# Block attention and a squared-ReLU MLP in one kernel: plain block products for groups 3 and 4, Strassen's scheme from group 5 on, and w_in's sums moved to VectorE

## The chip, the cores and the metric

The kernel runs on one core of one Trainium2 chip. The metric is the device time of one execution in microseconds (us), as the median of several executions. A second number is the span of one execution that was recorded by the hardware profiler; all rows of views below come from that execution.

## The reference

Two stages follow each other. Attention has 4 batches, 8 heads, 768 positions and 64 dimensions a head; a block mask lets a block of 32 queries see its neighbours, the first and last block and three sampled blocks. Its output, as 3072 rows of 512, is the input x of an MLP:

```python
h = x @ w_in                      # 3072 x 512 by 512 x 2048
r = np.maximum(h, 0.0)
g = s * (r * r) + b
return (g @ w_out).astype(np.float32)   # by 2048 x 512
```

The change concerns the MLP alone.

## The kernel before, in words

**Precision.** TensorE multiplies in a rounded format, so every operand is split into a high part (a rounded copy, made by ScalarE) and a low part (operand minus high part, made by VectorE or GpSimd), and every product is three matmuls: high by high, high by low, low by high. The weights arrive as 64-bit numbers and are decoded into the two parts by nine steps on VectorE and ScalarE (`decode_f64`, L75 to L85).

**Groups and blocks.** The 3072 rows of x make 8 groups of 384 rows, two for each batch. The hidden width 2048 makes 16 blocks f of 128. For a group g and a block f, `mlp1` (L399 to L401) makes 12 matmuls of 384 columns into a bank of PSUM; `relu` (ScalarE, L404), `square` (VectorE, L408), `hidden_high` (ScalarE, L412 and L413) and `hidden_low` (GpSimd, L417) make the two parts of the hidden block; `mlp2` (L438 to L440) makes 9 matmuls of 512 columns, which add it to the group's output in three PSUM banks. After a group's sixteenth block the three banks are copied to three buffers `ob` (ScalarE L444, VectorE L446) and stored. The pair g, f is called a sub below.

**First stage: the plan.** Attention, the decoding of the weights, and the first 30 subs of groups 1 and 2 (block by block, the two groups in turn) are ordered by a planner (class `Plan`) that walks over all steps with costs and priorities and then issues each engine's steps in the order found. Subs 31 and 32 follow by hand.

**Second stage: Strassen's scheme.** Groups 3 and 4, then 5 and 6, then 7 and 8 are done in pairs. Here w_in's block columns f and f+8 and its upper and lower half form a 2 by 2 matrix, x's two groups and two halves another, and seven products of six matmuls each (L1199) take the place of the eight that four subs need (48 matmuls). A pair of groups takes eight rounds, p = 0 to 7. A round makes the products in the order 1, 2, 6, 7, 5, 3, 4, with four blocks of `mlp2` between them (`out_block`). The operands are

```python
PAIRS = {1: ("A11", "B11"), 2: ("A12", "B21"), 3: ("S4", "B22"), 4: ("A22", "T4"),
         5: ("S1", "T1"), 6: ("S2", "T2"), 7: ("S3", "T3")}
```

The A are quarters of w_in, the B quarters of x; the S are sums of quarters of w_in, made anew each round (GpSimd, L1167), the T sums of quarters of x, made once for two groups (VectorE L1172, and T4 on GpSimd, L1169). Each operand is split into parts (`split`, ScalarE L1183, VectorE L1185). VectorE joins the products: `take` makes a hidden block from a product and an earlier sum (L1209) and squares it (L1210); L1266, L1268 and L1271 keep the sums between products.

**What sets the order there.** The engines work in the order in which the code issues. Small tables, `W_NOW`, `W_NEXT`, `X_NOW`, `X_NEXT` and `FIRST`, say after which product of which round a split (h or l and a name), a sum (+) or a load (<) is issued. Products use two PSUM banks in turn.

**w_in made whole.** Strassen's scheme needs w_in in one piece, so high and low part are added again (`win_sum`, GpSimd, L305) and a DMA writes the sum over the high part (`win_whole`, L309). That can be done for a block f once groups 1 and 2 are through with it. 24 of the 32 half blocks are done inside the plan, the other 8 in the first four rounds of groups 3 and 4.

Of the kernel before, what the change touches and what calls it, by code (L numbers as in the profile page):

```python
# [202 lines left out]
def kernel(  # L203
# [98 lines left out]
    def win_sum(f, h, tmp):  # L302

        a, b = (win(f, part)[:, h * NW // 2:(h + 1) * NW // 2].bitcast(F32) for part in range(2))
        nc.gpsimd.tensor_tensor(out=tmp, in0=a, in1=b, op=ALU.add)  # L305
# [75 lines left out]
    subs = [(g, f) for g in range(2) for f in range(2)] + [(g, f) for f in range(2, NFC) for g in range(2)]  # L381
    NSUB = len(subs)
# [44 lines left out]
    def mlp2(i, gf=None):  # L427
# [5 lines left out]
        for t in range(TG):  # L433
# [7 lines left out]
            if last:  # L441
                ob = wos["pool"].tile([P, DM], F32, tag="ob", name=f"ob{g}_{t}", bufs=3)
                if t % 2 == 0:
                    nc.scalar.copy(ob, acc)  # L444
                else:
                    nc.vector.tensor_copy(ob, acc)  # L446
# [10 lines left out]
    with ExitStack() as es:  # L457
# [418 lines left out]
        plan = Plan({"ws": 3, "kraw": RB, "qr": QB, "v": 4, "kg": 4, "vg": 2, "B": NBANK,  # L876
# [220 lines left out]
        hd, m2, last_of = {}, {}, {}  # L1097
        for k in range(NPL):
# [3 lines left out]
            last_of[f] = pm  # L1102
# [7 lines left out]

        for k in range(24):
            f, h = divmod(k, 2)
            o = op("g", 720, N + T["M1"] + 2 * f + 6 + 0.1 * h,
                   lambda f=f, h=h, k=k: win_sum(f, h, wos["x"][:, k % 3 * NW // 2:(k % 3 + 1) * NW // 2]), [last_of[f]], alloc=[("ws", k)], order=[wdone[("o", 8, 6)]])
            op("s", 450, N + T["M1"] + 2 * f + 7 + 0.1 * h,
               lambda f=f, h=h, k=k: win_whole(f, h, wos["x"][:, k % 3 * NW // 2:(k % 3 + 1) * NW // 2]), [o], use=[("ws", k)], nbytes=131e3)
# [45 lines left out]
    def add(p, n):  # L1162

        if n[0] == "S":
            a, b, how = {"S1": (quarter(p, "A21"), quarter(p, "A22"), ALU.add), "S2": (wsum["S1"], quarter(p, "A11"), ALU.subtract),
                         "S3": (quarter(p, "A11"), quarter(p, "A21"), ALU.subtract), "S4": (quarter(p, "A12"), wsum["S2"], ALU.subtract)}[n]
            gps.tensor_tensor(out=wsum[n], in0=a, in1=b, op=how)  # L1167
        elif n == "T4":
            gps.tensor_tensor(out=xsum[n], in0=xsum["T2"], in1=xsum[n], op=ALU.subtract)  # L1169
# [4 lines left out]
    def split(p, n, part):  # L1174
# [9 lines left out]
        else:  # L1184
            (gps if n == "B22" else vec).tensor_tensor(out=lo, in0=src, in1=hi.bitcast(F32), op=ALU.subtract)  # L1185
# [37 lines left out]
    def work(p, s, what):  # L1223

        for w in what.split():
# [4 lines left out]
            else:  # L1230
# [3 lines left out]
    W_NOW = {1: "lA22 lS4"}  # L1234
    W_NEXT = {1: "hA11", 2: "lA11 hA12", 6: "+S1 +S2 lA12", 7: "+S3 hS2", 5: "lS2 hS3 hS1", 3: "+S4 lS3 lS1", 4: "hA22 hS4"}
    X_NOW = {1: "lT4", 2: "hB22", 6: "lB22"}
    X_NEXT = {2: {1: "<T1 <T3 <T2 <T4"}, 6: {1: "+T3", 2: "+T1", 6: "+T2", 7: "+T4"},
              7: {1: "<B11", 2: "<B21", 6: "hT2", 7: "hB11 lT2 hT3", 5: "lB11 lT3 hT1 hB21", 3: "lT1 lB21 <B22", 4: "hT4"}}
    FIRST = {1: "hT3 hS3 lT3 lS3", 2: "hT1 hS1 lT1 lS1 +T4 +S4", 6: "hB22 hS4 lS4 lB22", 7: "hA22 hT4 lA22 lT4"}
    for i in range(NPL, NSUB):  # L1240
        if i == NPL:
            work(0, 1, "<B11 <B21 <T1 <T3 <T2 <T4")
        mlp1(i)
        relu(i)
# [3 lines left out]
        work(0, 1, "hB11 hA11 hB21 hA12" if i == NPL else "+T3 +S1 +S2 +T1 +T2 hT2 hS2")  # L1248
        hidden_high(i)
        hidden_low(i)  # L1250
        work(0, 1, "lB11 lA11 lB21 lA12" if i == NPL else "lT2 lS2 +S3 <B22")
        fifo.append((i, None))
    for s in range(1, B):
        a, b = 2 * s, 2 * s + 1
        for p in range(NFC // 2):
            for n in (1, 2, 6, 7, 5, 3, 4):
                to = product(n)
                i = None
                if n in (2, 4) and len(fifo) >= 3 or n == 2 and s == 1 and p == 0:
                    out_block()  # L1260
# [108 lines left out]
```

## Time and profile before

| | us |
|---|---|
| median of 3 runs (835.27 to 837.11) | 835.32 |
| profiled execution | 840.79 |
| its span, first to last instruction | 838.8 |
| PE busy in the span | 792.8 |
| VectorE (DVE) busy | 613.1 |
| ScalarE (ACT) busy | 506.0 |
| GpSimd (POOL) busy | 332.0 |
| mean granted TensorE clock | 0.977 |

PE is TensorE's matmul side. The mean that a row gives for one matmul includes its way through the array, and neighbours overlap: from one start to the next a matmul takes less. A granted clock of 1.00 is full speed.

### The profile page before, as it was taken

The page shows a single profiled execution, that of the slowest core. Times are in us where ns is not written, and L with a number is a line of the kernel's source. Part 1 is how long each engine was busy: PE and PEld are TensorE (multiplying, and loading weights), DVE is VectorE, ACT ScalarE, POOL GpSimd, SP SyncE. Part 2 cuts the span into 40 slices and gives each one's busy share as a digit, 9 for nine tenths or more (in the row PEclk, how much of TensorE's full clock was granted, in tenths as well). Part 3 has the DMA queues.
Part 4 walks back from the last instruction along what each step waited for, and adds up shares of the span by engine and source line. Part 5 has one row for each costly group of instructions (what it writes and reads, how often), then busy time and mean ns, then how long its engine had stood idle before and what let it go on. Part 6 is the DMA issues. An engine that isn't in the chain of part 4 may idle for free.

```text
span 838.8 us, 22214 instructions
## 1 busy us (share of the span) xinstructions
PE 792.8 (95%) x8368; PEld 682.7 (81%) x8368; DVE 613.1 (73%) x1400; ACT 506.0 (60%) x1200; POOL 332.0 (40%) x570
## 2 busy tenths in 40 slices
PE   7889999999999999998968999999999998999997
PEld 5567877888886889976867988978898997898896
DVE  4556778888978999999877666786666786655652
ACT  3556768778887787656654454456445464453552
POOL 1632124222400032575346455544544464345441
PEclk9899999999999999999978999999999999999999
DMA  8989797887777423444511200013100011100002
GB/s 231 230 227 317 213 251 213 237 242 220 210 209 235 140 81 122 137 155 135 162 56 51 87 14 14 0 57 107 45 0 1 1 40 53 41 1 1 2 1 75
DMA packets 87274, 96.80 MB, mean 115 GB/s; under 512 B 11392, under 2 KB 66176, under 8 KB 87168
## 3 DMA queue, kind: packets, MB, share of 16 engines
q1 hardware_dynamic: 87168, 95.39, 38.5%
q8 instruction: 66, 1.08, 0.6%
q14 instruction: 40, 0.33, 0.1%
HBM read 78.59 MB, written 12.58 MB: 109 GB/s over the span
## 4 chain that ended last, share of the span: by engine, by line
PE 70%; DVE 16%; DMA 5%; ACT 3%; issue 2%; SPq 2%; POOL 1%; DVEq 0%; ACTq 0%; POOLq 0%
PE m L1199 19%; PE o L439 8%; PE o L440 8%; PE o L438 8%; PE t L785 8%; PE xs L830 5%; PE s L708 4%; PE xs L844 3%; DMA kt<-in_k_seq_dram 2%; PE s L734 2%; DVE wklp L78 2%; DVE hid L408 2%; DVE wkhp L75 1%; PE s L722 1%; DVE wkhp L84 1%
## 5 line engine op out<-in xcount | busy, mean ns | idle before, releaser
L417 POOL TENSOR_TENSOR hid<-hid,hid 128x384 fp32r<-128x384 f32 x128 | 140.8, 1100 | 334.4 <-ACT hid L1217 178.9
L1216 ACT ACTIVATE hid<-hid,sb_b,sb_s 128x384 f32<-128x384 f32 x96 | 68.0, 709 | 124.4 <-DVE hid L1210 124.4
L761 ACT ACTIVATE ptile<-ptile,nm 128x352 f32<-128x352 f32 (+2 forms) x208 | 120.9, 584 | 31.7 <-DVE nm L749 30.7
L668 POOL COPY kg<-kt 128x128 f32 x264 | 63.8, 300 | 131.4 <-PE s L734 123.5
L1199 PE MATMUL m<-xT,wop 128*128 128x384 f32 x432 | 89.2, 342 | 5.7 <-DVE hid L1209 3.0
L749 DVE CUSTOM_DVE_ANT_0 ptile<-s,ms 128x352 f32<-128x352 f32 x160 | 74.3, 521 | 26.6 <-PE s L734 26.3
L1199 PE MATMUL m<-win 128*128 128x384 f32 x432 | 86.0, 343 | 7.7 <-DVE hid L1209 4.3
L1199 PEld LDWEIGHTS m<-win 128*128 128x128 f32 x432 | 78.5, 191 | 13.1 <-issue 4.9
L1199 PEld LDWEIGHTS m<-xT,wop 128*128 128x128 f32 x432 | 78.4, 191 | 8.6 <-issue 6.5
L785 PE MATMUL t<-ident,ptile 128*128 128x128 f32 x608 | 81.3, 283 | 1.2 <-ACT ptile L761 0.6
L438 PE MATMUL o<-wout,hid 128*128 128x512 f32 x192 | 75.9, 395 | 3.6 <-ACT ob L444 3.6
L440 PE MATMUL o<-woutr,hid 128*128 128x512 f32 x192 | 77.4, 403 | 0.0
L439 PE MATMUL o<-woutr,hid 128*128 128x512 f32 x192 | 77.3, 403 | 0.0
L440 PE MATMUL o<-wout,hid 128*128 128x512 f32 x192 | 76.8, 400 | 0.0
L439 PE MATMUL o<-wout,hid 128*128 128x512 f32 x192 | 76.8, 400 | 0.0
L438 PE MATMUL o<-woutr,hid 128*128 128x512 f32 x192 | 76.3, 397 | 0.0
L785 PEld LDWEIGHTS t<-ident,ptile 128*128 128x128 f32 x608 | 67.6, 144 | 7.7 <-ACT ptile L761 2.2
L1209 DVE TENSOR_TENSOR hid<-m,sum 128x384 f32<-128x384 f32 x48 | 26.7, 556 | 61.5 <-PE m L1199 59.6
L789 DVE COPY pt<-t 128x384 f32<-128x384 f32 (+1 forms) x104 | 56.3, 545 | 13.0 <-PE t L785 10.3
L791 ACT COPY pt<-t 128x384 f32<-128x384 f32 (+1 forms) x104 | 48.8, 473 | 24.9 <-PE t L785 24.3
L1210 DVE SCALAR_TENSOR_TENSOR hid<-hid 128x384 f32<-128x384 f32 x96 | 54.9, 572 | 3.3
L1185 DVE TENSOR_TENSOR wop<-win,wop 128x256 fp32r<-128x256 f32 x24 | 27.6, 1149 | 37.5 <-ACT wop L1183 37.5
(168 smaller groups left out, 1742.4 us busy)
## 6 DMA issues: line engine op xcount, KB each, us to landing
vg<-in_v_dram SPq DMA_DIRECT2D x136, 128.0 KB, 3.6
v<-in_v_sta_dram SPq DMA_DIRECT2D x40, 256.0 KB, 5.2
kt<-in_k_seq_dram SPq DMA_DIRECT2D x16, 544.0 KB, 7.8
raw_i<-in_w_in_dram SPq DMA_DIRECT2D x16, 512.0 KB, 4.2
raw_o<-in_w_out_dram SPq DMA_DIRECT2D x16, 512.0 KB, 3.3
v<-in_v_dram SPq DMA_DIRECT2D x16, 384.0 KB, 6.7
xd<-xst SPq DMA_DIRECT2D x44, 128.0 KB, 4.0
out_dram<-ob SPq DMA_DIRECT2D x20, 256.0 KB, 2.0
```

The source lines that it names most:

```text
L417: nc.gpsimd.tensor_tensor(out=htile(5 + i % 3), in0=t, in1=gh.bitcast(F32), op=ALU.subtract)
L438: nc.tensor.matmul(acc, gh[:, tsl], wout(f, 0), start=first, stop=False)
L439: nc.tensor.matmul(acc, gh[:, tsl], wout(f, 1), start=False, stop=False)
L440: nc.tensor.matmul(acc, gl[:, tsl], wout(f, 0), start=False, stop=last)
L668: nc.gpsimd.tensor_copy(kg[:, m], kts[b][:, :, bass.ds(box["js"][m], BLK)])
L749: nc.vector.tensor_tensor_reduce(out=pt[:, :w], in0=sps.pop((n, g))[:, :w], in1=msk, scale=-scale, scalar=FMAX if g == 0 else nm[:, 0:1], ...
L761: nc.scalar.activation(pt[:, :w], pt[:, :w], AF.Exp, bias=nms[n][:, last:last + 1], scale=-1.0, accum_out=dns[i][:, g, j:j + 1])
L785: nc.tensor.transpose(tp[:, c, :], src[:, c * P:(c + 1) * P], ident)
L789: nc.vector.tensor_copy(to, src)
L1199: nc.tensor.matmul(to, w_, x_, start=(c == 0 and k == 0), stop=(c == 1 and k == 2))
L1210: vec.scalar_tensor_tensor(out=t, in0=t, scalar=0.0, in1=t, op0=ALU.max, op1=ALU.mult)
L1216: nc.scalar.activation(t, t, AF.Identity, bias=sb_b, scale=sb_s)
```

## The change

- `subs` gets 32 more entries: groups 3 and 4 are done block by block as groups 1 and 2 are, with x loaded and split for them at subs 31 to 33 (`xload`, `xsplit`). Strassen's scheme starts at groups 5 and 6 (`S0 = 2`).
- `win_sum` runs on VectorE. The 24 sums and their DMAs leave the plan; 30 of the 32 are made in every second sub of groups 3 and 4 (a block is summed when both groups are through with it), the last two just ahead of the first product.
- The sums S and T4 run on VectorE too. GpSimd keeps `hidden_low` and the low part of T4; the low part of B22 goes to VectorE.
- The operands of the first round are prepared in subs 55 to 64 (table `EARLY`, indices 54 to 63), four splits of it in the first round itself (`FIRST`). In the other rounds the tables put steps elsewhere: the T sums lie in rounds 4 and 5 in place of round 6, and of the six low parts of x (768 columns, on VectorE) three lie in the last round of a pair of groups and three in the first of the next.
- For all groups but the last two, the three copies to `ob` are all made by ScalarE.

```diff
-        nc.gpsimd.tensor_tensor(out=tmp, in0=a, in1=b, op=ALU.add)
+        nc.vector.tensor_tensor(out=tmp, in0=a, in1=b, op=ALU.add)
...
+    subs += [(g, f) for f in range(NFC) for g in range(2, 4)]
...
-                if t % 2 == 0:
+                if t % 2 == 0 or b < B - 1:
                     nc.scalar.copy(ob, acc)
...
-        for k in range(24):
-            f, h = divmod(k, 2)
-            o = op("g", 720, N + T["M1"] + 2 * f + 6 + 0.1 * h,
-                   lambda f=f, h=h, k=k: win_sum(f, h, wos["x"][:, k % 3 * NW // 2:(k % 3 + 1) * NW // 2]), [last_of[f]], alloc=[("ws", k)], order=[wdone[("o", 8, 6)]])
-            op("s", 450, N + T["M1"] + 2 * f + 7 + 0.1 * h,
-               lambda f=f, h=h, k=k: win_whole(f, h, wos["x"][:, k % 3 * NW // 2:(k % 3 + 1) * NW // 2]), [o], use=[("ws", k)], nbytes=131e3)
...
-            gps.tensor_tensor(out=wsum[n], in0=a, in1=b, op=how)
+            vec.tensor_tensor(out=wsum[n], in0=a, in1=b, op=how)
         elif n == "T4":
-            gps.tensor_tensor(out=xsum[n], in0=xsum["T2"], in1=xsum[n], op=ALU.subtract)
+            vec.tensor_tensor(out=xsum[n], in0=xsum["T2"], in1=xsum[n], op=ALU.subtract)
...
-            (gps if n == "B22" else vec).tensor_tensor(out=lo, in0=src, in1=hi.bitcast(F32), op=ALU.subtract)
+            (gps if n == "T4" else vec).tensor_tensor(out=lo, in0=src, in1=hi.bitcast(F32), op=ALU.subtract)
...
-    X_NOW = {1: "lT4", 2: "hB22", 6: "lB22"}
+    X_NOW = {1: "hT4 hB22", 2: "lT4 lT3", 7: "lT1", 5: "lB22"}
...
-    FIRST = {1: "hT3 hS3 lT3 lS3", 2: "hT1 hS1 lT1 lS1 +T4 +S4", 6: "hB22 hS4 lS4 lB22", 7: "hA22 hT4 lA22 lT4"}
+    FIRST = {1: "hT4", 2: "lT4", 7: "hB22", 5: "lB22"}
...
         mlp1(i)
+        if i in (31, 32):
+            for c in range(NCC):
+                xsplit(i - 29, c)
+        if i == 31:
+            for c2 in range(2):
+                xload(3, c2)
         relu(i)
         if i - LAG >= NPL - 1:
             mlp2(i - LAG)
         square(i)
...
+        if i > 33 and i % 2 == 0:
+            for h in range(2):
+                tmp = wos["x"][:, (i + h) % 3 * NW // 2:((i + h) % 3 + 1) * NW // 2]
+                win_sum((i - 34) // 2, h, tmp)
+                win_whole((i - 34) // 2, h, tmp)
         hidden_high(i)
         hidden_low(i)
...
+        work(0, S0, EARLY.get(i, ""))
...
-    for s in range(1, B):
+    for s in range(S0, B):
```

**GpSimd at the end of the plan.** Before, sums of w_in's parts (`xrest<-win`) stand between the steps that make the low part of a hidden block (`hid`); hid4 in, hid7 out and so on are its buffers.

```order
L417 TENSOR_TENSOR hid6_7129<-hid1_7088,hid3_7113 128x384
L305 TENSOR_TENSOR xrest_7563<-win0_3301 128x256 x3
L417 TENSOR_TENSOR hid7_7139<-hid0_7051,hid4_7125 128x384
L305 TENSOR_TENSOR xrest_7563<-win0_3301 128x256
L417 TENSOR_TENSOR hid5_7092<-hid1_7088,hid2_7077 128x384
L305 TENSOR_TENSOR xrest_7563<-win0_3301 128x256 x3
```

Now, at the same place:

```order
L419 TENSOR_TENSOR hid6_7129<-hid1_7088,hid3_7113 128x384
L419 TENSOR_TENSOR hid7_7139<-hid0_7051,hid4_7125 128x384
L419 TENSOR_TENSOR hid5_7092<-hid1_7088,hid2_7077 128x384
L419 TENSOR_TENSOR hid6_7129<-hid0_7051,hid3_7113 128x384
L419 TENSOR_TENSOR hid7_7139<-hid1_7088,hid4_7125 128x384
```

All 24 sums are gone from there. Up to the end of the plan the rows of TensorE, VectorE and ScalarE are the same in both kernels.

**VectorE in the first round of Strassen's scheme.** Before (groups 3 and 4); `xT` and `xB` are parts of x's operands, `wop` and `win` of w_in's, `m` the products, of which m2 is the third and m3 the fourth.

```order
L1185 TENSOR_TENSOR xT1_8298<-sum0_8181,xT1_8298 128x3x2x128
L1185 TENSOR_TENSOR wop0_8179<-sum0_8181,wop0_8179 128x256
L1185 TENSOR_TENSOR win0_3301<-win0_3301 128x256
L1266 TENSOR_TENSOR xrest_7563<-m2_8310,xrest_7563 128x384
L1185 TENSOR_TENSOR wop1_8180<-sum3_8184,wop1_8180 128x256
L1185 TENSOR_TENSOR win1_5488<-win0_3301,win1_5488 128x256
L1268 TENSOR_TENSOR sum4_8185<-m3_8325,xrest_7563 128x384
L1185 TENSOR_TENSOR wop1_8180<-win2_7437,wop1_8180 128x256
L1185 TENSOR_TENSOR xT4_8334<-sum3_8184,xT4_8334 128x3x2x128
```

Now (groups 5 and 6), up to the step that takes the sixth product, m5:

```order
L1280 TENSOR_TENSOR xrest_7563<-m2_9252,xrest_7563 128x384
L1282 TENSOR_TENSOR sum4_8137<-m3_9261,xrest_7563 128x384
L1179 TENSOR_TENSOR win1_5488<-win0_3301,win1_5488 128x256
L1179 TENSOR_TENSOR win2_7437<-sum2_8135,win2_7437 128x256
L1161 TENSOR_TENSOR sum1_8134<-win0_3301,win2_7437 128x256
L1203 TENSOR_TENSOR hid1_7088<-m4_9292,sum4_8137 128x384
L1204 SCALAR_TENSOR_TENSOR hid1_7088<-hid1_7088 128x384
L1285 TENSOR_TENSOR sum4_8137<-m4_9292,xrest_7563 128x384
L1179 TENSOR_TENSOR xB22_9200<-xB22_9200 128x768
L1161 TENSOR_TENSOR sum3_8136<-win0_3301,sum2_8135 128x256
L1203 TENSOR_TENSOR hid0_7051<-m5_9309,sum4_8137 128x384
```

The parts of the round's own operands are gone from the row but for xB22, which the sixth product reads and which stands behind three steps on the fifth product, m4. The S sums (L1161) have come in from GpSimd.

**VectorE from the last round of groups 5 and 6 into the first of groups 7 and 8.** Before, from the fifth product of that last round (m109) on:

```order
L1271 TENSOR_TENSOR sum4_8185<-m109_10341,xrest_7563 128x384
L1185 TENSOR_TENSOR win2_7437<-sum2_8183,win2_7437 128x256
L1185 TENSOR_TENSOR win0_3301<-win0_3301 128x768
L1185 TENSOR_TENSOR xT3_8265<-sum1_8182,xT3_8265 128x3x2x128
L1209 TENSOR_TENSOR hid0_7051<-m110_10370,sum4_8185 128x384
L1210 SCALAR_TENSOR_TENSOR hid0_7051<-hid0_7051 128x384
L1185 TENSOR_TENSOR wop0_8179<-sum1_8182,wop0_8179 128x256
L1185 TENSOR_TENSOR wop0_8179<-sum0_8181,wop0_8179 128x256
L1185 TENSOR_TENSOR xT1_8298<-sum0_8181,xT1_8298 128x3x2x128
L1185 TENSOR_TENSOR win1_5488<-win1_5488 128x768
L1209 TENSOR_TENSOR hid1_7088<-sum4_8185,m111_10388 128x384
```

Now, from the same place (m53 is the fifth product of that round):

```order
L1285 TENSOR_TENSOR sum4_8137<-m53_10193,xrest_7563 128x384
L1179 TENSOR_TENSOR win2_7437<-sum2_8135,win2_7437 128x3x2x128
L1161 TENSOR_TENSOR sum3_8136<-win0_3301,sum2_8135 128x256
L1203 TENSOR_TENSOR hid0_7051<-m54_10220,sum4_8137 128x384
L1204 SCALAR_TENSOR_TENSOR hid0_7051<-hid0_7051 128x384
L1203 TENSOR_TENSOR hid1_7088<-sum4_8137,m55_10233 128x384
L1204 SCALAR_TENSOR_TENSOR hid1_7088<-hid1_7088 128x384
L1179 TENSOR_TENSOR win1_5488<-win1_5488 128x768
```

Four steps of 768 columns (two on `win`, two on `xT`) stood ahead of the take of the seventh product, m111; now one stands ahead of the take of the seventh, m55, and the next 768 columns come behind it.

More of the change, by code (lines that the diff above doesn't have):

```diff
@@ L873, in spill @@
             nc.sync.dma_start(out=to, in_=xst)
-        plan = Plan({"ws": 3, "kraw": RB, "qr": QB, "v": 4, "kg": 4, "vg": 2, "B": NBANK,
+        plan = Plan({"kraw": RB, "qr": QB, "v": 4, "kg": 4, "vg": 2, "B": NBANK,
                      "o": 1, "P": len(ptiles), "pt": 5, "xst": 4, "xss": 2, "nm": 10, "dn": 5,
@@ L1096 @@
         pm, pm2 = o_m, None
-        hd, m2, last_of = {}, {}, {}
+        hd, m2 = {}, {}
         for k in range(NPL):
@@ L1101 @@
                 pm = op("p", 490, N + T["M1"] + k, lambda k=k, c=c: mlp1(k, (c,)), cols=1152, deps=[*ends, xs_ops[(g, c, 1)], wdone[("i", f, 8)], hd.get((k - 2, 0))], order=[pm])
-            last_of[f] = pm
             dep = pm
@@ L1247 @@
         square(i)
-        work(0, 1, "hB11 hA11 hB21 hA12" if i == NPL else "+T3 +S1 +S2 +T1 +T2 hT2 hS2")
+        if i > 33 and i % 2 == 0:
[3 more added lines that the diff above has]
+                win_whole((i - 34) // 2, h, tmp)
         hidden_high(i)
         hidden_low(i)
-        work(0, 1, "lB11 lA11 lB21 lA12" if i == NPL else "lT2 lS2 +S3 <B22")
-        fifo.append((i, None))
-    for s in range(1, B):
+        work(0, S0, EARLY.get(i, ""))
+        if i >= NSUB - LAG:
+            fifo.append((i, None))
+    for h in range(2):
+        win_sum(NFC - 1, h, wsum["v"])
+        win_whole(NFC - 1, h, wsum["v"])
+    for s in range(S0, B):
         a, b = 2 * s, 2 * s + 1
@@ L1258 @@
                 i = None
-                if n in (2, 4) and len(fifo) >= 3 or n == 2 and s == 1 and p == 0:
+                if n in (2, 4) and len(fifo) >= 3 or n == 2 and s == S0 and p == 0:
                     out_block()
@@ L1275 @@
                     i = take((a, p + 8), u["u2"], to, ALU.subtract)
-                if s == 1 and p == 0:
+                if s == S0 and p == 0:
                     work(p, s, FIRST.get(n, ""))
                 else:
-                    work(p, s, W_NOW.get(n, ""))
                     if p == 0:
                         work(p, s, X_NOW.get(n, ""))
+                    work(p, s, W_NOW.get(n, ""))
                 if i is not None:
                     finish(i)
+                if s < B - 1:
+                    work(p, s + 1, X_NEXT.get(p, {}).get(n, ""))
                 if s < B - 1 or p < NFC // 2 - 1:
                     work((p + 1) % (NFC // 2), s + 1, W_NEXT.get(n, ""))
-                if s < B - 1:
-                    work(p, s + 1, X_NEXT.get(p, {}).get(n, ""))
                 if n == 7 and len(fifo) >= 2 or n == 5 and len(fifo) >= 3:
                     out_block()
-            if s == 1 and p < 4:
-                for h in range(2):
-                    win_sum(12 + p, h, wsum["v"])
-                    win_whole(12 + p, h, wsum["v"])
     while fifo:
```

15 lines of the change are left out of this document (10 added, 5 removed).

## The prediction

> **What bounds the kernel now.** I read the busy time by stretches first, then the waits of TensorE (PE), then the row of products. In the stretches the columns after the window are its length, busy us and count of PE, PEld, DVE, ACT and POOL, then granted clock, DMA share and GB/s.
>
> ```profile
> 340.00:400.00 60.00, 54.19 (x259) 47.12 (x258) 58.10 (x74) 37.80 (x67) 37.49 (x36) 0.98 0.47 149
> 422.00:462.00 40.00, 30.53 (x130) 26.46 (x129) 31.95 (x44) 21.48 (x45) 23.15 (x22) 0.83 0.16 56
> ...
> 586.00:680.00 94.00, 94.00 (x468) 84.57 (x468) 62.05 (x112) 46.37 (x99) 47.14 (x51) 1.00 0.04 15
> ```
>
> PE sets the pace nearly everywhere: from 586 to 680 it is never idle, at full clock, with VectorE (DVE) busy two thirds of the time. Three places differ: the end of the plan (340 to 400), where VectorE is busy 97% and PE loses 5.8 us; the first round of Strassen's scheme (422 to 462), where PE loses 9.5 us and the clock falls to 0.83; and the change from groups 5 and 6 to groups 7 and 8. PE's waits from 330 us on name who holds it (total, times, longest):
>
> ```profile
> PE m L1199 <- DVE hid L1209: 7.3, 3, 3.0
> PE h L399 <- ACT hid L404: 5.7, 4, 2.0
> PE o L438 <- ACT ob L444: 3.6, 2, 2.9
> PE m L1199 <- ACT xrest L1262: 3.4, 1, 3.4
> PE m L1199 <- DVE sum L1271: 2.6, 1, 2.6
> ```
>
> These make 22.6 us. Each wait costs more than itself when the clock follows. The timeline of PE after one wait, and when the half rate ends (start, duration, instruction):
>
> ```profile
> 396.06 0.44 PE L399 MATMUL h<-x,win 128*128 128x384 f32 x1 [2.03 <-ACT hid L404]
> ...
> 397.60 0.52 PE L400 MATMUL h<-x,win 128*128 128x384 f32 x1
> 397.92 0.52 PE L401 MATMUL h<-x,win 128*128 128x384 f32 x1
> ...
> 400.48 0.44 PE L438 MATMUL o<-woutr,hid 128*128 128x512 f32 x1
> ...
> 401.91 0.34 PE L399 MATMUL h<-x,win 128*128 128x384 f32 x1
> 402.09 0.34 PE L400 MATMUL h<-x,win 128*128 128x384 f32 x1
> ...
> 406.08 0.33 PE L399 MATMUL h<-x,win 128*128 128x384 f32 x1
> ```
>
> From 397.28 or so to 400.48 a 384-column matmul takes 0.32 us from start to start, later 0.18: a wait of 2.03 us cost another 1.6 us. The last two first matmuls show a sub's length with PE always at work, 406.08 - 401.91 = 4.17 us.
>
> The products show where rounds and pairs of groups begin. The rows are the first products of groups 3 and 4, of their rounds 1 and 2, of groups 5 and 6 and their round 1, and of groups 7 and 8 and their round 1:
>
> ```profile
> 424.80 2.27 PE L1199 MATMUL m<-win 128*128 128x384 f32 x12
> ...
> 453.03 2.27 PE L1199 MATMUL m<-win 128*128 128x384 f32 x12
> ...
> 468.74 1.57 PE L1199 MATMUL m<-win 128*128 128x384 f32 x8
> ...
> 562.98 1.22 PE L1199 MATMUL m<-win 128*128 128x384 f32 x6
> ...
> 583.74 2.26 PE L1199 MATMUL m<-win 128*128 128x384 f32 x12
> ...
> 693.68 1.22 PE L1199 MATMUL m<-win 128*128 128x384 f32 x6
> ...
> 718.03 2.26 PE L1199 MATMUL m<-win 128*128 128x384 f32 x12
> ```
>
> A good round takes 468.74 - 453.03 = 15.71 us. The first rounds take 28.23, 20.76 and 24.35 us. So the pairs take 138.18 us (562.98 - 424.80) and 130.70 us (693.68 - 562.98), where eight good rounds would be 125.7.
>
> **Plan.** What the sums on GpSimd (POOL) do to VectorE, in the timelines of DVE and of POOL:
>
> ```profile
> 356.47 1.27 DVE L84 TENSOR_SCALAR wkhp<-woutr 128x512 int32<-128x512 int32 x1
> 357.77 1.11 DVE L85 SCALAR_TENSOR_TENSOR woutr<-wklp,wkhp 128x512 fp32r<-128x512 f32 x1
> 358.81 1.22 DVE L78 SCALAR_TENSOR_TENSOR wklp<-wklp,raw_i 128x512 f32<-128x512 int32 x1
> ...
> 361.54 0.43 DVE L84 TENSOR_SCALAR wkhp<-win 128x512 int32<-128x512 int32 x1
> ...
> 367.54 0.69 DVE L85 SCALAR_TENSOR_TENSOR woutr<-wklp,wkhp 128x512 fp32r<-128x512 f32 x1
> ...
> 377.52 0.68 DVE L78 SCALAR_TENSOR_TENSOR wklp<-wklp,raw_o 128x512 f32<-128x512 int32 x1
> ```
>
> ```profile
> 356.44 1.02 POOL L417 TENSOR_TENSOR hid<-hid,hid 128x384 fp32r<-128x384 f32 x1 [1.70 <-ACT hid L413]
> 357.41 2.07 POOL L305 TENSOR_TENSOR xrest<-win 128x256 f32<-128x256 f32 x2
> ```
>
> Beside three POOL steps the three DVE steps lost 0.84 + 0.42 + 0.54 = 1.8 us, 0.6 us for each step. 24 sums leave, so VectorE gets some 14 us back of the 58 it was busy. PE's waits there (the second row of waits, 5.7 us) are for `relu`, whose buffers come free through VectorE and POOL, so they go, and the 1.6 us of half clock with them: 7.3 us at most, since PE's own work cannot shrink. I take -6.5, because VectorE with some 44 us of work left in 60 still needs three quarters of PE's time there, in a fixed order; ends -4 and -7.3.
>
> **Groups 3 and 4.** At 424.80 two subs of groups 1 and 2 still lack their block of `mlp2`; at the first product of groups 5 and 6 two subs of groups 3 and 4 will. Between lie 32 subs of 4.17 us, 133.5 us. Eight good rounds are 125.7, so the plain products cost 7.8 us more of PE, and this is paid in full; the loss of the first round goes. New is the change of x behind sub 31: eight copies on ScalarE and eight differences on VectorE. The buffers for the first half come free with sub 31's matmuls; PE then still has sub 32's matmuls and one block of `mlp2`, 4.17 us together, and four differences at about 0.55 us (row 447.59 below, same width) behind the first copy end just in time. Behind these copies on ScalarE stand the `relu` of subs 32 and 33 and six copies to `ob` at 0.54 us (row 708.71 below), so ScalarE is nearly full for three subs. I take 0.5 us lost, ends 0 and 4. The win sums lie beside PE's work: a sub gives VectorE a square and on average one sum, about 1 us of 4.17. 134.0 for 138.18: -4.2.
>
> **Groups 5 and 6, first round.** Its operands are ready but for four splits. One counts: xB22's low part, behind the take of the fifth product and the kept sum, in front of the sixth product's matmuls. DVE rows for these steps:
>
> ```profile
> 437.19 0.54 DVE L1209 TENSOR_TENSOR hid<-m,xrest 128x384 f32<-128x384 f32 x1
> 437.77 0.56 DVE L1210 SCALAR_TENSOR_TENSOR hid<-hid 128x384 f32<-128x384 f32 x1
> 438.24 0.95 DVE L1185 TENSOR_TENSOR xT<-sum,xT 128x768 fp32r<-128x768 f32 x1
> 439.11 0.42 DVE L1185 TENSOR_TENSOR wop<-sum,wop 128x256 fp32r<-128x256 f32 x1
> ...
> 447.59 0.55 DVE L1271 TENSOR_TENSOR sum<-m,xrest 128x384 f32<-128x384 f32 x1
> ```
>
> Take 1.05 (437.19 to 438.24), kept sum 0.5, split 0.95, some 0.4 for two hand-overs: 2.9 us after the fifth product. In this round no block of `mlp2` is there to cover it (three blocks, not four), so PE waits about 3.0 us and, by the row at 396.06, loses 1.6 us of clock: 13.7 (15.71 less a block of `mlp2`, 4.17 - 12 x 0.18 = 2.0) + 4.6 = 18.3 for 20.76, -2.5. Ends: no wait -7.1, a wait of 7 us +1.
>
> In words, the Trainium skill's page TensorE: Matmul & The Clock Gate (What's actually happening) has the clock fall only after an idle window of about 3.4 us. The row at 396.06 disagrees, with half rate after 2.03 us; by the rule this term would be -4.1.
>
> **Groups 7 and 8, first round.** It lost 24.35 - 15.71 = 8.6 us: one of the three waits for a take (7.3 / 3 = 2.4 us each), behind four wide steps; the longest wait for a copy to `ob`, 2.9 us; the rest clock. The ACT timeline shows why the copies came late:
>
> ```profile
> 708.40 0.41 ACT L1183 CAST win<-sum 128x256 fp32r<-128x256 f32 x1 [4.38 <-POOL sum L1167]
> 708.71 1.07 ACT L444 COPY ob<-o 128x512 f32<-128x512 f32 x2
> ...
> 713.64 0.59 ACT L444 COPY ob<-o 128x512 f32<-128x512 f32 x1 [2.10 <-DMA out_dram<-ob]
> ```
>
> ScalarE stood 4.38 us for a POOL sum, copied two outputs only then, and the next three waited for the stores. The S sums now come early on VectorE, where a 256-column step takes 0.42 us, and the wide steps lie three and three. What is left is xB22's low part again, 2.9 us after the fifth product, this time behind a block of 2.0 us: 0.9 us, with POOL beside it 1.3. Too short for the clock. 17.0 for 24.35: -7.3; ends -8.6 and -4.
>
> **The steady rounds.** Four S sums of 0.42 us join VectorE's 62.05 / 94 x 15.71 = 10.4 us of a round: 12.1 of 15.7, and less where POOL no longer stretches it. That is hidden by PE's 15.71 us; nothing.
>
> **The sum.** -6.5 - 4.2 - 2.5 - 7.3 = -20.5: span 838.8 to 818.3, the profiled execution 840.79 to 820.3. The median of the runs shown is 5.5 us under the profiled execution; the same 20.5 off 835.32 gives 814.8 us.
>
> **The rivals.** *The loss at the entry only moves.* VectorE and ScalarE have as many sums and splits to do ahead of the first products; if `EARLY` backs up behind late loads of x, groups 5 and 6 lose in their first round what groups 3 and 4 lost, 28.23 - 13.7 = 14.5 us, not 4.6. For it: five loads of x go out together only in sub 57, and VectorE's first step on them is two subs later. Against: VectorE's share, nine wide steps at 0.95 us and eleven narrow at 0.42 us, is 13.2 us and stands in six subs, 25.0 us, beside some 6 us of squares and win sums. 814.8 + 9.9 = 824.7 us.
>
> *The plan does not get shorter.* PE's waits there might hang on decoding alone and not on POOL. For it: VectorE is busy 97%. Against: the stretched rows. 814.8 + 6.5 = 821.3 us.
>
> *The clock holds* after the wait of 3 us: 814.8 - 1.6 = 813.2 us. For it: half rate comes in stretches of some 3 us (397.28 to 400.48), and the wait may lie across two of them. Against: 2.03 us were enough at 396.06. The clock-gate rule named above stands behind this rival.
>
> *Slower: VectorE becomes the bound of Strassen's rounds.* In each of the 16 rounds that are left the four sums stand in VectorE's row between takes, where a split waiting for ScalarE holds them all. At 2 us a round it is 32 us: 846.8 us. It decides from 20.5 / 16 = 1.28 us a round, 17.0 us in all. For it: sums on POOL took 0.77 to 0.91 us each, and at double VectorE's price they would leave 2 us of slack. Against: 12.1 us of work and PE idle nowhere from 586 to 680. The sums' POOL price in rows:
>
> ```profile
> L1167 POOL TENSOR_TENSOR sum<-win 128x256 f32<-128x256 f32 x24 | 21.9, 911 | 0.0
> ...
> L1167 POOL TENSOR_TENSOR sum<-win,win 128x256 f32<-128x256 f32 x24 | 18.5, 772 | 0.0
> ```
>
> The Trainium skill's page Perfetto Trace Analysis (Optimizing Scalar/DVE Operations) would, with VectorE saturated, send work to GpSimd, the other way than this change; it adds that the two share a read port, so that it might not help. VectorE's 66% in the rounds speaks against saturation there.
>
> **How the numbers follow.** Forecast 0.58, entry loss moves 0.12, plan no shorter 0.10, clock holds 0.13, VectorE-bound 0.07. A measurement of this kernel can tell about 0.3%, 2.5 us, from no change. All but the last are faster by far; of the last 0.06 is slower and 0.01 within 0.3%, and I leave 0.01 more for within, for terms that fail together: faster 0.92, same 0.02, slower 0.06. The bounds of the terms add up to -27.7 and -7, which seldom meet; the range 808.5 to 825 takes in all rivals but the slow one.
>
> **What would show it.** Right: no wait of PE for `relu` from 340 to 400; VectorE's decode steps at 0.43 and 0.69 us there; first product of groups 5 and 6 near 552 us; one wait of about 3 us before the sixth product of their first round; first round of groups 7 and 8 near 17 us; other rounds 15.7. Wrong: rounds over 16 us (VectorE as bound), subs of groups 3 and 4 over 4.3 us, a first round over 24 us, or the first product of groups 5 and 6 after 560 us.

## The result, and the profile after

The changed kernel takes 822.93 us (median of 4 runs, 819.56 to 824.55); the kernel before, run beside it, 835.3 us (835.0 to 837.11). The ratio is 0.984, with a 95% interval of 0.981 to 0.988: 10 to 16 us faster. The forecast was 814.8 us, with a range of 808.5 to 825. The profiled execution of the changed kernel took 822.26 us, its span 820.5 us; against 840.79 and 838.8 that is 18.5 and 18.3 us less. The difference of the medians is smaller, and the reason is the first thing to see.

The first matmul of the MLP, in the row of PE's matmuls, of the kernel before and then of the changed one (start, duration, instruction):

```profile
283.31 0.42 PE L399 MATMUL h<-x,win 128*128 128x384 f32 x1
```

```profile
281.36 0.42 PE L401 MATMUL h<-x,win 128*128 128x384 f32 x1
```

Ahead of it lies attention, with the same TensorE order in all kernels of this study. In twelve further profiled executions it came at 277.09 to 288.12 us. So up to 11 us of an execution is decided before the changed part begins, and medians of four runs move by several us. Behind it the stages repeat closely: from the first matmul of the MLP to the first product of groups 5 and 6 it took 267.00 to 267.05 us in the changed kernel and in its nine variants. I therefore compare stages, and quote times beside them.

The changed kernel's row of products, with the start of sub 33, the first of groups 3 and 4, ahead of it. The products are the first of groups 5 and 6, of their rounds 1 and 2, and of groups 7 and 8 and their round 1:

```profile
413.96 0.34 PE L401 MATMUL h<-x,win 128*128 128x384 f32 x1
...
548.41 2.27 PE L1193 MATMUL m<-win 128*128 128x384 f32 x12
...
571.23 2.27 PE L1193 MATMUL m<-win 128*128 128x384 f32 x12
...
586.93 2.27 PE L1193 MATMUL m<-win 128*128 128x384 f32 x12
...
681.17 2.27 PE L1193 MATMUL m<-win 128*128 128x384 f32 x12
...
699.44 2.27 PE L1193 MATMUL m<-win 128*128 128x384 f32 x12
```

The same stages side by side, from one profiled execution each:

| stage | before, us | after, us | measured | forecast |
|---|---|---|---|---|
| attention, to the first matmul of the MLP | 283.31 | 281.36 | -1.95 | 0 |
| from there to the first step of groups 3 and 4 | 141.49 | 132.60 | -8.9 | -6.5 |
| groups 3 and 4 | 138.18 | 134.45 | -3.7 | -4.2 |
| groups 5 and 6 | 130.70 | 132.76 | +2.1 | -2.5 |
| groups 7 and 8, first round | 24.35 | 18.27 | -6.1 | -7.3 |

Without attention the terms give -16.6 us, where the forecast had -20.5. The steady rounds are the same: 586.93 - 571.23 = 15.70 us.

PE's waits of the changed kernel from 330 us on (total, times, longest):

```profile
PE m L1193 <- DVE hid L1203: 3.8, 1, 3.8
PE m L1193 <- DVE xB L1179: 2.8, 2, 2.5
PE m L1193 <- DVE xT L1179: 1.4, 2, 1.0
PE h L402 <- DVE x L374: 0.2, 1, 0.2
```

They sum to 8.2 us where the five rows of before sum to 22.6. The waits for `relu`, for the copies to `ob` and for the kept sum (L1271 before) are gone. The largest that is left, 3.8 us for a take (L1203), stands ahead of the fourth product of the first round of Strassen's scheme. The kernel before waited for a take at the same product, as its row and then the changed kernel's show; what makes the take late is new:

```profile
437.88 2.26 PE L1199 MATMUL m<-xT,wop 128*128 128x384 f32 x6 [3.03 <-DVE hid L1209]
```

```profile
557.62 2.29 PE L1193 MATMUL m<-xT,wop 128*128 128x384 f32 x6 [3.79 <-DVE hid L1203]
```

Busy times of the changed kernel in four stretches (columns as in the prediction):

```profile
340.00:400.00 60.00, 60.00 (x303) 54.32 (x302) 57.38 (x93) 45.55 (x82) 16.32 (x14) 1.00 0.32 105
...
600.00:660.00 60.00, 60.00 (x300) 53.97 (x299) 45.37 (x89) 27.84 (x60) 16.13 (x16) 1.00 0.00 1
```

```profile
548.00:571.00 23.00, 16.75 (x72) 14.51 (x70) 14.65 (x27) 12.99 (x25) 5.08 (x5) 0.85 0.47 159
557.00:561.00 4.00, 3.38 (x10) 3.10 (x11) 3.74 (x10) 2.57 (x5) 1.02 (x1) 0.50 0.60 229
```

From 340 to 400 PE is busy throughout, and VectorE still 96%: it does more steps in the same time (93 where there were 74). In the first round of groups 5 and 6 PE is idle 6.25 of 23 us, and from 557 to 561 the clock is 0.50; the half rate lasts from 556.11 to 562.94 us. What holds the take there is in VectorE's own row, with GpSimd's beside it:

```profile
550.62 2.06 DVE L1179 TENSOR_TENSOR xT<-sum,xT 128x768 fp32r<-128x768 f32 x2 [1.97 <-ACT xT L1177]
552.60 2.05 DVE L305 TENSOR_TENSOR sum<-win 128x256 f32<-128x256 f32 x1
556.67 0.43 DVE L305 TENSOR_TENSOR sum<-win 128x256 f32<-128x256 f32 x1 [2.02 <-DMA win<-sum]
557.01 0.55 DVE L1203 TENSOR_TENSOR hid<-m,xrest 128x384 f32<-128x384 f32 x1
```

```profile
552.50 1.86 POOL L1179 TENSOR_TENSOR xT<-sum,xT 128x768 fp32r<-128x768 f32 x1 [1.51 <-ACT xT L1177]
```

The last two of w_in's sums stand ahead of the first take. The first takes 2.05 us in place of 0.4, while GpSimd makes T4's low part; the second writes to the same buffer and waits until the DMA has stored the first. The take, due at about 552.6, starts at 557.01.

### The profile page after: what moved, and what is told of

The parts are those of the page before. It is cut to its first block, busy times and chain, and to the rows that moved or that the text cites. A ratio compares the mean times of both kernels' runs of the same rounds, so it can differ in the third digit from the quotient of the medians.

```text
span 820.5 us, 22018 instructions
## 1 busy us (share of the span) xinstructions
PE 790.8 (96%) x8416; PEld 685.8 (84%) x8416; DVE 558.7 (68%) x1379; ACT 494.5 (60%) x1175; POOL 213.7 (26%) x438
## 4 chain that ended last, share of the span: by engine, by line
PE 82%; DMA 6%; DVE 4%; issue 3%; ACT 3%; SPq 1%; POOL 0%; ACTq 0%; DVEq 0%; POOLq 0%
PE m L1193 13%; PE o L441 10%; PE o L442 10%; PE o L440 9%; PE t L787 8%; PE xs L832 5%; PE s L710 5%; PE h L402 4%; PE h L403 4%; PE h L401 4%; PE xs L846 3%; PE s L736 2%; DMA kt<-in_k_seq_dram 2%; DMA vg<-in_v_dram 2%; PE s L724 1%
## 5 line engine op out<-in xcount | busy, mean ns | idle before, releaser
L419 POOL TENSOR_TENSOR hid<-hid,hid 128x384 fp32r<-128x384 f32 x128 | 138.5, 1083 | 448.8 <-ACT hid L415 253.5
L1210 ACT ACTIVATE hid<-hid,sb_b,sb_s 128x384 f32<-128x384 f32 x64 | 45.3, 708 | 119.2 <-DVE hid L1204 119.1
L410 DVE SCALAR_TENSOR_TENSOR hid<-hid,sb_s 128x384 f32<-128x384 f32 x64 | 41.5, 649 | 88.4 <-ACT hid L406 88.3
L401 PE MATMUL h<-x,win 128*128 128x384 f32 x256 | 86.5, 338 | 0.6 <-ACT hid L406 0.6
L402 PE MATMUL h<-x,win 128*128 128x384 f32 x256 | 86.1, 336 | 0.2 <-DVE x L374 0.2
L403 PE MATMUL h<-x,win 128*128 128x384 f32 x256 | 86.3, 337 | 0.0
L442 PE MATMUL o<-woutr,hid 128*128 128x512 f32 x192 | 76.4, 398 | 0.0
L441 PE MATMUL o<-woutr,hid 128*128 128x512 f32 x192 | 76.4, 398 | 0.0
L442 PE MATMUL o<-wout,hid 128*128 128x512 f32 x192 | 75.9, 395 | 0.0
L441 PE MATMUL o<-wout,hid 128*128 128x512 f32 x192 | 75.8, 395 | 0.0
L440 PE MATMUL o<-woutr,hid 128*128 128x512 f32 x192 | 75.3, 392 | 0.0
L440 PE MATMUL o<-wout,hid 128*128 128x512 f32 x192 | 74.7, 389 | 0.0
L1193 PE MATMUL m<-xT,wop 128*128 128x384 f32 x288 | 59.7, 341 | 5.2 <-DVE hid L1203 3.8
L406 ACT ACTIVATE hid<-h 128x384 f32<-128x384 f32 x64 | 31.1, 486 | 52.4 <-PE h L403 49.3
L414 ACT ACTIVATE hid<-hid,sb_b 128x384 f32<-128x384 f32 x64 | 39.3, 615 | 37.7 <-DVE hid L410 37.7
```

What stands on the lines that cost most here:

```text
L401: nc.tensor.matmul(ph, wh, xh, start=(c == 0), stop=False)
L402: nc.tensor.matmul(ph, wh, xl, start=False, stop=False)
L403: nc.tensor.matmul(ph, wl, xh, start=False, stop=(c == NCC - 1))
L419: nc.gpsimd.tensor_tensor(out=htile(5 + i % 3), in0=t, in1=gh.bitcast(F32), op=ALU.subtract)
L440: nc.tensor.matmul(acc, gh[:, tsl], wout(f, 0), start=first, stop=False)
L441: nc.tensor.matmul(acc, gh[:, tsl], wout(f, 1), start=False, stop=False)
```

## The experiments

Stages are given as a length from the first matmul of the MLP, or as the length of a round; "first round" is that of groups 5 and 6 unless said otherwise. Two theories stood against each other at each place where the forecast was off or its reason untested: for the plan, stretched VectorE steps against decoding that is slow anyway; for the entry, the two sums against the splits of x; for groups 7 and 8, the S sums against the copies and against the places of x's low parts.

**The kernel before, profiled again** (no edit).

> The kernel before, profiled once more, unchanged. Its first profiled execution was 840.79 us, 5.5 us over its median, and the forecast took 20.5 us off both. If that execution lost the 5.5 us in attention, whose code is the same in both kernels, the first matmul of the MLP comes at 278 to 281 us here in place of 283.31 and the stages behind it last as before within 0.5 us (135.2 us from there to sub 31, 138.2 for groups 3 and 4, 130.7 for 5 and 6). If it lost them in the waits that the change removes, attention is as long as before and those stages are together some 5 us shorter.

It took 839.66 us. The first matmul of the MLP came at 281.29; from there to the first product 140.96 us, groups 3 and 4 138.21, groups 5 and 6 132.37. So attention accounts for 2 us of the difference between executions and the later stages repeat within 2 us; the kernel's runs beside the experiments spread from 833.76 to 843.25 us. Neither case as expected: the first profiled execution was not unusual, the four runs of its first comparison lay low.

**Before, without the plan's sums** (the sums and stores are left out, so w_in is not made whole).

```diff
-        for k in range(24):
-            f, h = divmod(k, 2)
-            o = op("g", 720, N + T["M1"] + 2 * f + 6 + 0.1 * h,
...
```

> The kernel before without the 24 sums of w_in's parts in the plan and their DMAs: w_in stays split for those blocks, so this leaves work out and its output differs. Theory: these sums on GpSimd stretch VectorE's decoding, and PE's waits for relu come from that. Then PE has no wait from 340 us to the end of the plan, the stretch from the first matmul of the MLP to sub 31 takes 126.3 us as in the changed kernel (before: 135.2), groups 3 and 4 stay at 138 us, and the time is 826 to 828 us. Rival, PE waits for the decoding itself: 135 us and 835 us.

829.27 us, ratio 0.990 (0.987 to 0.993) to the kernel before. The first matmul of the MLP and the first product:

```profile
277.09 0.42 PE L399 MATMUL h<-x,win 128*128 128x384 f32 x1
...
409.66 2.27 PE L1193 MATMUL m<-win 128*128 128x384 f32 x12
```

132.57 us, 8.9 less than before and equal to the changed kernel's 132.60. PE has no wait there, and the long waits at the entry of groups 3 and 4 stay (3.4, 4.0 and 2.6 us). The plan's whole term comes from these 24 sums, with their stores. Without them VectorE's same 186 steps, from the first matmul of the MLP to sub 31, are busy 115.7 us in place of 127.3.

**Before, the sums on VectorE and still in the plan.**

```diff
-        nc.gpsimd.tensor_tensor(out=tmp, in0=a, in1=b, op=ALU.add)
+        nc.vector.tensor_tensor(out=tmp, in0=a, in1=b, op=ALU.add)
...
-            o = op("g", 720, N + T["M1"] + 2 * f + 6 + 0.1 * h,
+            o = op("v", 380, N + T["M1"] + 2 * f + 6 + 0.1 * h,
```

> The kernel before with all of w_in's sums on VectorE and still in the plan; TensorE's order is unchanged. It parts the two halves of the first edit: the sums leave GpSimd, but not the plan. VectorE gets back 14 us of stretch and takes on 24 sums of 0.35 to 0.42 us, 8.4 to 10 us. Theory, VectorE's time is the bound there: the stretch from the first matmul of the MLP to the first product takes 136 to 140 us (before 141.2, without the sums 132.6). Rival, it is GpSimd's row that held up the low parts of the hidden blocks: 132 to 134 us.

831.04 us (one run); 138.08 us to the first product, as the theory had it. PE's waits in that stretch now name the decoding steps:

```profile
PE o L439 <- DVE woutr L85: 1.5, 1, 1.5
PE h L401 <- DVE win L85: 1.3, 1, 1.3
```

Of the 8.9 us, 3.4 come from taking the sums off GpSimd and 5.5 from taking them out of the stage in which VectorE is full; there VectorE also waited 1.6 us for the stores of earlier sums.

**The changed kernel, its sums on GpSimd.**

```diff
-        nc.vector.tensor_tensor(out=tmp, in0=a, in1=b, op=ALU.add)
+        nc.gpsimd.tensor_tensor(out=tmp, in0=a, in1=b, op=ALU.add)
```

> The changed kernel with w_in's sums on GpSimd again, at their new places in groups 3 and 4. Theory: what counts is that they left the plan, where VectorE is full; in groups 3 and 4 VectorE is busy about a third, so stretching it costs nothing: 267.0 us from the first matmul of the MLP to the first product as with VectorE, within 0.7 us. And with the last two sums out of VectorE's row the wait of 3.79 us goes, so the first round of groups 5 and 6 falls to 16 to 19 us. Rival, the engine is what counts: the stretch up to the first product grows by 3 us or more.

824.62 us (one run). 267.03 us to the first product, within 0.03 us that of the changed kernel: in groups 3 and 4 the engine does not matter, the place does. The first round fell only to 20.60 us, less than expected: the 3.8 us wait became 0.67, but waits of 0.31 and 0.87 us came up beside it, and behind the wait for xB22 the clock was 0.50 for 3.41 us, some 1.7 us of PE's time, which the next run does not lose.

**The last two sums later.** In the changed kernel, behind rounds 0 and 1.

```diff
-    for h in range(2):
-        win_sum(NFC - 1, h, wsum["v"])
-        win_whole(NFC - 1, h, wsum["v"])
...
+            if s == S0 and p < 2:
+                win_sum(NFC - 1, p, wsum["v"])
+                win_whole(NFC - 1, p, wsum["v"])
```

> The changed kernel with the last two of w_in's sums moved from ahead of the first product to behind rounds 0 and 1 of groups 5 and 6, one each. Theory: they stand in VectorE's row ahead of the first take, the second waits 2.02 us for the store of the first because both use one buffer, and so the fourth product waits 3.79 us. Then that wait falls under 0.5 us, the first round from 22.8 to about 17.5 us, and the time by 5 us, to 817 to 819 us. Rival, the take is late because of the splits of x ahead of it: the round stays above 21 us, the time within 1.5 us of the changed kernel's.

816.62 us, ratio 0.975 (0.968 to 0.982) to the kernel before. VectorE's row and PE's products of that round:

```profile
548.86 2.06 DVE L1179 TENSOR_TENSOR xT<-sum,xT 128x768 fp32r<-128x768 f32 x2 [1.97 <-ACT xT L1177]
550.84 0.55 DVE L1203 TENSOR_TENSOR hid<-m,xrest 128x384 f32<-128x384 f32 x1
```

```profile
546.66 2.27 PE L1193 MATMUL m<-win 128*128 128x384 f32 x12
...
558.90 1.15 PE L1193 MATMUL m<-xB,wop 128*128 128x384 f32 x5 [2.46 <-DVE xB L1179]
...
563.02 1.23 PE L1193 MATMUL m<-win 128*128 128x384 f32 x6
```

The take of the first round follows the splits of x at once, and the round takes 563.02 - 546.66 = 16.36 us, 6.5 less than 22.82. The rival falls: the same splits stand ahead of the take. The clock stayed at 1.00 in this round, behind a wait of 2.46 us.

**Two buffers.** In the changed kernel, the second sum in a buffer of its own, both still ahead of the take.

```diff
-        win_sum(NFC - 1, h, wsum["v"])
-        win_whole(NFC - 1, h, wsum["v"])
+        tmp = wsum["v"] if h == 0 else xsum["u"][:, HALF:HALF + HN]
+        win_sum(NFC - 1, h, tmp)
+        win_whole(NFC - 1, h, tmp)
```

> The changed kernel with a second buffer for the second of w_in's last two sums, which both stay ahead of the first take. Theory: of the take's lateness 2.02 us is the wait for the store and some 1.6 us the stretch of the first sum beside GpSimd's low part of T4. Then the fourth product waits 1 to 2 us in place of 3.79, and the first round of groups 5 and 6 takes 19.5 to 21 us (22.82 in the changed kernel, 16.36 with the sums moved). Rival, the splits of x ahead of the sums hold the take: the wait stays above 3 us.

820.01 us (one run); the wait is 1.69 us and the round 19.85 us, both as the theory had them. So the buffer is worth 3.0 of the 6.5 us and the place ahead of the take 3.5, but not all of this is the wait itself. Of the idle time, 3.79 us, the buffer takes 2.1 and the place 1.7. The rest is mostly half clock: 6.83 us of it in the changed kernel, 3.41 us here, behind the wait for xB22, and none in the run with the sums moved.

**B22's low part earlier.** In the changed kernel, behind the fourth product.

```diff
-    X_NOW = {1: "hT4 hB22", 2: "lT4 lT3", 7: "lT1", 5: "lB22"}
+    X_NOW = {1: "hT4 hB22", 2: "lT4 lT3", 7: "lT1 lB22"}
...
-    FIRST = {1: "hT4", 2: "lT4", 7: "hB22", 5: "lB22"}
+    FIRST = {1: "hT4", 2: "lT4", 7: "hB22 lB22"}
```

> The changed kernel with the low part of B22 made after the fourth product in place of after the fifth, in both first rounds. Theory: the sixth product waits for that step alone, behind the take and the kept sum of the fifth. Then the wait of 2.46 us in the first round of groups 5 and 6 falls under 0.6 us and that of 0.38 us in groups 7 and 8 goes; the time falls by 2.5 to 4 us. Rival, the step only pushes the take of the fifth product back: the wait moves to the seventh product and the time stays within 1 us.

818.69 us, ratio 0.975 (0.969 to 0.981). The wait for B22 goes from both first rounds, but the seventh product now waits 0.72 us, and the rounds take 21.12 and 17.95 us in place of 22.82 and 18.27: 2.0 us in all, short of the 2.5 to 4. Both theories had a part of it.

**Both edits.**

> The changed kernel with both edits: the last two sums behind rounds 0 and 1, and the low part of B22 ahead of the take of the fifth product. Moved alone, the sums took 6.5 us off the first round of groups 5 and 6 and B22's low part 1.7 us, and 0.3 us off that of groups 7 and 8. If the two are separate waits, the first round takes 14.5 to 15 us, the span from the first matmul of the MLP to the last of TensorE 525 to 526 us (533.9 in the changed kernel), and the time is 8 to 9 us under the changed kernel's. If one stands in for the other, the gain stays at 6.5 us.

815.55 us, ratio 0.971 (0.967 to 0.974). The first round takes 15.86 us, only 0.5 under 16.36: the wait for B22 falls from 2.46 to 0.30 us and the seventh product waits 1.39 us. One wait stood in for the other, as the second case had it. From the first matmul of the MLP to TensorE's last it is 526.58 us, 7.3 less than the changed kernel's 533.92.

**Both edits, and an output block ahead of the seventh product.**

```diff
+                if n == 4 and s == S0 and p == 0:
+                    out_block()
                 to = product(n)
```

> The kernel with both edits (last two sums later, B22's low part earlier), and the third output block of the first round of groups 5 and 6 ahead of the seventh product in place of behind it. The seventh product waited 1.39 us for the kept sum of the fifth, with no block to cover it. Theory: the block covers it, the first round falls from 15.86 to 14.2 to 14.6 us, the span from the first matmul of the MLP to TensorE's last from 526.6 to about 525 us, the time by 1.4 us, which the time alone can hardly show. Rival, the block itself waits for its hidden part: no gain.

815.9 us, ratio 0.972 (0.969 to 0.976). The first round takes 14.19 us, but the next one 16.74 in place of 15.7, and the span is 525.98 us: 0.6 us won of 1.4. This and the run above are the fastest versions found; their times do not tell them apart.

**S sums on GpSimd.** In the changed kernel, for S and T4.

```diff
-            vec.tensor_tensor(out=wsum[n], in0=a, in1=b, op=how)
+            gps.tensor_tensor(out=wsum[n], in0=a, in1=b, op=how)
```

> The changed kernel with the S sums and T4 back on GpSimd, everything else as changed. Theory: in the steady rounds PE covers them on either engine, 15.71 us, but in the first round of groups 7 and 8 ScalarE waits for them again and the copies of the outputs come late: that round goes from 18.27 to 20 us or more, that of groups 5 and 6 from 22.8 to 24 us or more, the time up by 3 to 6 us. Rival, the new places in the tables alone made the gain of groups 7 and 8: both rounds stay within 0.7 us. A third, VectorE as the bound of the rounds: the steady rounds get shorter than 15.7 us.

824.42 us, ratio 0.982 (0.977 to 0.988). The first round rose to 25.36 us as expected, that of groups 7 and 8 did not: 18.09 us. The steady rounds stayed at 15.71, so VectorE is no bound there. ScalarE's row in the first round of groups 7 and 8:

```profile
695.23 0.41 ACT L1177 CAST win<-sum 128x256 fp32r<-128x256 f32 x1 [2.98 <-POOL sum L1161]
695.54 1.55 ACT L446 COPY ob<-o 128x512 f32<-128x512 f32 x3
```

The wait for the sum is back and the copies are late, but PE does not wait for them. My theory falls.

**Copies to `ob` shared again.** In the changed kernel, the middle copy on VectorE for all groups.

```diff
-                if t % 2 == 0 or b < B - 1:
+                if t % 2 == 0:
```

> The changed kernel with the middle one of the three copies to ob on VectorE again for all groups. With the S sums on GpSimd the first round of groups 7 and 8 stayed at 18.1 us, though ScalarE waited 2.98 us for a sum again. Theory: the copies are what removed the wait for the bank there, since the copy on VectorE stood behind stores and ahead of takes. Then a wait of PE for ob of 1 us or more comes back in that round, and it takes 20 to 23 us in place of 18.27. Rival, the places of x's low parts made the gain alone: the round stays within 0.7 us of 18.27.

825.79 us (one run). That round took 18.49 us: the rival's case.

**x's low parts in the last round.** In the changed kernel.

```diff
-    X_NOW = {1: "hT4 hB22", 2: "lT4 lT3", 7: "lT1", 5: "lB22"}
+    X_NOW = {1: "hT4 hB22", 2: "lT4", 5: "lB22"}
...
-              7: {1: "<B11", 2: "<B21", 6: "hB11", 7: "lB11 hT2 hB21", 5: "lT2 hT3", 3: "<B22", 4: "lB21 hT1"}}
+              7: {1: "<B11", 2: "<B21", 6: "hB11", 7: "lB11 hT2 hB21", 5: "lT2 hT3", 3: "lT3 <B22", 4: "lB21 hT1 lT1"}}
```

> The changed kernel with the low parts of T3 and T1 back in the last round of groups 5 and 6, so that five of six stand there as before. Theory: three and three removed the wait for the take at the change of groups. Then PE waits 1 to 3 us around the first two products of groups 7 and 8, and the last round of groups 5 and 6 and the first of 7 and 8 take together 35 to 38 us (15.70 + 18.27 = 33.97 in the changed kernel). Rival, the spread does not matter: together within 0.7 us of 33.97.

820.73 us (one run). The two rounds took 15.71 and 18.31 us, together 34.02: no change. How many wide steps lie in which round does not matter by itself; the waits only moved to other products of that round.

## Why the prediction was right, and where it was not

**The time** lay in the range and the sign was right, but the time is 8 us over the forecast. About half of that is the sum of the terms (-16.6 for -20.5). Most of the rest came from setting the sum off the median of few runs: they gave 835.3 us, and beside the experiments the medians of the same kernel were 838.23 to 839.0 us. The profiled execution was the better base: there the forecast of the span, 818.3 us, missed by 2.2 us. Part of that nearness is luck: 1.95 us of the measured difference are attention, which the forecast had at nothing, and the plan's 2.4 us more than forecast offset half of the 4.6 us that the term of groups 5 and 6 missed by. The upper bounds of the terms, -4, -0.7, +1 and -4, add up to -7.7, not to the -7 written; nothing else was worked out from it.

**Plan, -6.5.** The mechanism is shown: without the 24 sums and their stores, and with nothing else changed, the stage is 8.9 us shorter, and VectorE's other steps there shrink by 11.6 us (14 forecast). The size was low, and the bound of 7.3 us was no bound. I had added PE's recorded idle time, 5.7 us, and the half clock, 1.6 us. Summed from start to start against 0.174 us for a 384-column and 0.229 us for a 512-column matmul, the kernel before lost 9.7 us between 320 and 418 us, the changed one 0.7 in its stretch up to sub 31: each stop costs some 0.3 us more than its idle time. At 396.06, 2.20 us are lost ahead of the matmul where 2.03 are recorded as idle, because the matmul ahead of the stop still counts as busy for the time that its successor would have overlapped (a 512-column matmul is recorded with 0.40 us, while the next one starts 0.23 us after it). The first matmul behind the stop costs another 0.1 us: its successor starts 0.28 us after it in place of 0.174.

**Groups 3 and 4, -4.2.** Right: 134.45 us for 134.0. At 32 subs that is 4.20 us for one, and the change of x costs a wait of 0.2 us.

**Groups 5 and 6, first round, -2.5.** This step failed, and with it the sign of the term. The wait for xB22 was there, 2.46 us for the 3.0 forecast. The step that I had not counted is the pair of sums ahead of the first take. I had written that the win sums lie beside PE's work; that holds for 30 of them, while the last two stand in front of the round's first take and share one buffer. The rival "the loss at the entry only moves" had the place right and the cause wrong: 22.82 - 13.7 = 9.1 us were lost, between the 4.6 of the forecast and its 14.5, and `EARLY` was not late enough to cost anything. The splits for the first product were done before it began, and the two of x that run on for some 4 us into the round delay no product in the run with the sums moved.

**Half clock.** The clock was 0.50 for 6.83 us around the end of the wait of 3.79 us. In the run with the sums moved it stayed at 1.00 behind 2.46 us. In the kernel before it fell behind 2.03 us, but in the second profile of that same kernel the same wait, 2.03 us ahead of the same matmul, left it at 1.00. My taking 2.03 us as enough was too simple, and the traces show more. From 330 us on, every stretch at half rate except the one at the kernel's end lasts 3.41 us, or two or three times that, and within one execution they start whole multiples of 3.41 us apart (397.14, 431.27, 448.34 and 567.81 us in the kernel before). So what counts is how much idle time falls into one such window. Here are the window with the wait of 2.03 us and the next one, of the kernel before and then of its second profile (columns as in the prediction):

```profile
393.73:397.14 3.41, 1.38 (x8) 1.08 (x7) 2.37 (x5) 3.38 (x8) 1.00 (x1) 1.00 0.10 37
397.14:400.55 3.41, 3.41 (x12) 3.12 (x11) 3.34 (x6) 3.03 (x7) 1.02 (x1) 0.50 0.48 154
```

```profile
392.32:395.74 3.42, 1.75 (x10) 1.75 (x11) 2.34 (x5) 3.36 (x8) 1.00 (x1) 1.00 0.00 0
395.74:399.15 3.41, 3.41 (x19) 3.02 (x18) 3.38 (x5) 2.99 (x6) 1.06 (x1) 1.00 0.46 154
```

In the first the whole wait lies in one window, in the second 1.67 us of it. Counted like this in all fourteen profiles, each of the 27 full-rate windows in which PE waited 1.91 us or more was followed by half rate; of the 24 in which it waited 0.95 to 1.84 us only two were, with 1.50 and 1.74 us. The rival "the clock holds" is therefore a matter of where a wait falls. What the Trainium skill's page TensorE: Matmul & The Clock Gate says (What's actually happening), that the window runs freely, lasts about 3.4 us and brings the half rate when it was idle, agrees with these stretches, except that a window idle for 1.91 us was enough here.

**Groups 7 and 8, first round, -7.3.** The size came near (-6.1), and the losses that I named are gone: the wait for a take, 2.15 us there, the wait for `ob`, 2.88 us, and the half clock behind each. What took them away is not shown. The S sums, the copies to `ob` and the places of x's low parts were each put back alone, and the round stayed at 18.1 to 18.5 us. What is left is not what I forecast either: of the 1.8 us of waits, 0.38 is for xB22, and 0.96 and 0.43 are for two of x's low parts that the change itself put into this round. For what went, two readings remain, argued and not shown. One is that the order within the round counts: before, wide steps stood in front of the take of the seventh product, as VectorE's row of the kernel before has it:

```profile
693.83 0.95 DVE L1185 TENSOR_TENSOR xT<-sum,xT 128x768 fp32r<-128x768 f32 x1
694.70 1.75 DVE L1185 TENSOR_TENSOR win<-win 128x768 fp32r<-128x768 f32 x1
696.37 0.54 DVE L1209 TENSOR_TENSOR hid<-sum,m 128x384 f32<-128x384 f32 x1
```

In the changed kernel the takes of the sixth and the seventh product follow each other and such steps come behind them; the run with the low parts in the last round put only one, of 0.95 us, between the two. The other is that the wait for `ob` is partly chance: in the four profiled executions with the code of before at that place it was 2.88, 2.67, 2.94 and 0.67 us, and in the last of them the round took 20.76 us in place of 24.35. So some 3.6 us of the measured 6.1 can come and go without the change, and the nearness to -7.3 is in part luck. No run puts the order of before back whole; this stays open.

**Steady rounds, nothing.** Right: 15.70 us, with the S sums on either engine. That refutes the slow rival, and in the run with the sums on GpSimd the steady rounds were no shorter.

## What to carry to other kernels

When a change moves work to an engine with room, look for the few instances that land at a seam: the 30 sums inside a stage cost nothing, the last two, in front of the first step of the next stage and through one buffer, cost 6.5 us, half clock included. Price a wait from start to start of the instructions around it, not by the idle time that the profile records. And where an early stage of the same code varies by more than the change is worth, compare stages from a landmark behind it, and use the medians only as a check. Before you credit a change with a whole round, profile the unchanged kernel twice: its round may vary by itself, and so may the clock behind the same wait.

## What the hardware showed that I had not expected

- Attention, with the same TensorE order, ended 277.09 to 288.12 us after the start, while the 267 us behind it repeated within 0.05 us.
- A VectorE sum of 256 columns, which takes 0.43 us in the row of the second one, took 2.05 us beside a GpSimd step of 1.86 us: it lost nearly all of the other's length. In the plan VectorE's steps lost 11.6 us to 24 GpSimd sums, some 0.5 us for each.
- The same wait of 2.03 us, in the same kernel, halved the clock in one execution and left it at 1.00 in another. The half rate came in stretches of 3.41 us or a multiple of that, and one followed each full-rate window of that length in which PE waited 1.91 us or more.
